# All engines' orders written out for the two MLP passes of a gated Fourier-mixing kernel

## The chip, the cores and the metric

The kernel runs on one core of one Trainium2 chip. The metric is the device time of one execution in microseconds, in fp32 throughout. The core has five engines that matter here: TensorE (PE in the profile; its weight loads are PEld), VectorE (DVE), ScalarE (ACT), GpSimd (POOL) and SyncE (SP). PE multiplies, DVE and ACT do elementwise work, SP only issues DMA transfers; POOL does here nothing but issue the transfers that add x to a tile. Each engine has its own list of instructions and waits for the others through semaphores.

## The reference, cut to what matters

```python
xn = layernorm(x)                                   # S, D = 2048, 512
a, b = xn @ dft_hid_re.T, xn @ dft_hid_im.T
s = dft_seq_re @ a - dft_seq_im @ b                 # Fourier mixing
h = relu(xn @ w1 + b1) ** 2                         # F = 1792
g = silu(h @ w2 + b2)
out = x + s * g
```

## The kernel before, in words

All matmuls work on pairs: a number is split into a high part (rounded to the matmul's fp32r type, ScalarE, line 67) and the low rest (VectorE, line 68), and each product takes the three passes high-high, high-low and low-high (PASSES). The large products are done in 2x2 blocks by a Strassen-Winograd scheme with seven products instead of eight (PRODUCTS, lines 33 to 55): sums of blocks are formed before (`sums_a`, `sums_b`), and the seven results M1 to M7 are put together after (`combine`, line 210). `combine` first copies M1 out of PSUM with ScalarE (L214) and then runs four VectorE additions (L215 to L218).

The kernel has three stages.

1. The sequence DFT (lines 300 to 613): eight chunks of 256 frequencies, ending near 419 us. Its results Y go to DRAM (`stage2`).
2. MLP pass one, `hidden`: 28 units, unit n = 7c + p for the token chunk c (4 chunks of 512 tokens) and the pair p of blocks of the hidden width (7 pairs). A unit is 42 matmuls (7 products x 2 halves x 3 passes, L474), the combine into a tile `h`, relu with b1 (L481, twice), square (L482) and a store of h to DRAM (HD, L483). Odd units use the PSUM tiles b3 and bc, even ones b2, ba and bb. In even units products 2 and 6 lie in ba, 7, 5, 3 and 4 in b2; in odd units these six lie in b3; product 1 lies in bb or bc.
3. MLP pass two, `outer`: again 28 units, 42 matmuls each (L523), which sum over p into seven PSUM tiles of chunk c (M1 in bb, M2 and M6 in b2, M7, M5 and M3 in b3, M4 in ba). Three of the tiles start from b2 (the bias): ScalarE writes it there (`bias`, L516, BIASED) ahead of the products 2, 5 and 4. After p = 6 the chunk is combined into `e` (called z in the profile), and in the next chunk's first units `finish` runs on the four parts k of z: silu (L548), times Y (L549), a transfer of GpSimd that adds x from DRAM into the tile (L552), and its store (L553). The last chunk's end is written out apart (lines 718 to 752): its last three units run product by product, and the end (`finishing`) adds x with VectorE and stores with SP.

Beside these matmuls run helpers, written as generators whose steps are placed by name with `go`: `x2` to `x7` (`xt_half`: load a raw token tile, L284; subtract the mean and multiply by the inverse deviation, L290; form sums; split), `m1` to `m3` (load the rows of means and deviations, L277), `w0`, `w4` to `w6` (`late_w2`: load a raw w2 tile, L432; form sums; split; store to DRAM, L448), `l1` to `l6` (load a finished w2 tile from DRAM, L427), and `h0` to `h27` (`operand`: load h from HD, L494; form sums; split). `beside` holds for each unit of pass one the steps ahead of it and behind it; in pass two each unit n does a step of h(n+3), h(n+2) and h(n+6).

`tc.manual_schedule` at line 618 makes VectorE and SP issue in the order in which the program is written. PE, ACT and POOL get their order from the compiler's scheduler, except in the last three units, where PE's is written too. Buffers have few homes: e (one), t (two), r (three), g1a, g1b, xc0 to xc7, wd0, wd1 and pq00 to pq11 are used by several of these steps in turn, so a load also waits until its home's former reader is done. The home of z is e: the next z can only be written when all four stores of the former z are done.

Of the kernel before, what the change touches and what calls it, by code (L numbers as in the profile page):

```python
# [9 lines left out]
AF = mybir.ActivationFunctionType  # L10
# [8 lines left out]
TC = 512  # L19
# [41 lines left out]
def fnet_gated_kernel(ctx, tc, x, xt, ct, wd, w1, w2, b1, b2, out):  # L61
# [145 lines left out]
        m26, m753, m4, m1 = ms  # L207
        return {1: m1, 4: m4, 2: m26[:, 0], 6: m26[:, 1], 7: m753[:, 0], 5: m753[:, 1], 3: m753[:, 2]}[n]

    def combine(e, ms):  # L210

        m26, m753, m4, m1 = ms
        pair = [P, 2, m1.shape[-1]]
        nc.scalar.activation(e[:, 0], m1, AF.Copy)  # L214
        nc.vector.tensor_tensor(e[:, 1:3], m26, e[:, 0:1].to_broadcast(pair), op=ALU.add)  # L215
        nc.vector.tensor_tensor(e[:, 0:4:3], m753[:, 0:2], e[:, 2:3].to_broadcast(pair), op=ALU.subtract)
        nc.vector.tensor_tensor(e[:, 2:4], m753[:, 1:3], e[:, 0:4:3], op=ALU.add)  # L217
        nc.vector.tensor_tensor(e[:, 0], m4, e[:, 0], op=ALU.subtract)  # L218
# [236 lines left out]
    def hidden(n, c, p):  # L455

        if n % 2:
            t, o = bank("b3", f"hps{n}_3"), bank("bc", f"hps{n}_1")
            t = t.rearrange("p a (b n) -> p (a b) n", n=256)
            ms = t[:, 0:2], t[:, 2:5], t[:, 5], o[:, 0, 0:256]  # L460
            order = ORDER
        else:
            t, u, o = (bank(tag, f"hps{n}_{tag}") for tag in ("b2", "ba", "bb"))
            t, u = (v.rearrange("p a (b n) -> p (a b) n", n=256) for v in (t, u))
            ms = u, t[:, 0:3], t[:, 3], o[:, 0, 0:256]
            order = ORDER if n else (1, 7, 5, 3, 4, 2, 6)
        first = set()
        for k in order:
            a, b = W1_SLOT[PRODUCTS[k][0]], B_SLOT[PRODUCTS[k][1]]

            share = next((pair for pair in ((2, 6), (7, 5), (3, 4)) if k in pair), k)
            for q in range(2):
                for a_, b_ in PASSES:
                    nc.tensor.matmul(product(ms, k), W1[p][a][:, a_, q * P:(q + 1) * P], xT[c, q][:, b_, b],  # L474
                                     start=share not in first, stop=q == 1 and (a_, b_) == (LO, HI),
                                     skip_group_check=True)
                    first.add(share)
        x_ = room(n, f"h{c}_{p}")
        combine(x_, ms)
        for f, s in ((2 * p, slice(C11, 4, 2)), (2 * p + 1, slice(C21, 4, 2))):  # L480
            nc.scalar.activation(x_[:, s], x_[:, s], AF.Relu, bias=b1s[:, f:f + 1])  # L481
        nc.scalar.activation(x_, x_, AF.Square)  # L482
        nc.scalar.dma_start(HD[c, p], x_)  # L483

    def operand(n, c, p):

# [43 lines left out]
    def at(src, k):  # L530

        h, b = WHERE[k]
        return src.rearrange("(h k p) (b e) -> h b p k e", h=2, k=2, b=2)[h, b]
# [11 lines left out]
    def finish(c, e, k):  # L545

        z = e[:, k]
        nc.scalar.activation(z, z, AF.Silu)  # L548
        nc.vector.tensor_tensor(z, z, fin[c][k // 2][:, k % 2], op=ALU.mult)  # L549
        z = z.rearrange("p (k e) -> p k e", e=256)  # L550
        tokens = slice(c * TC, (c + 1) * TC)
        nc.gpsimd.dma_start(z, at(x[tokens], k), accum_op=ALU.add)  # L552
        nc.gpsimd.dma_start(at(out[tokens], k), z)  # L553

    def finishing(c, e, k, cols=slice(0, 2)):

# [58 lines left out]
    units = [(c, p) for c in range(NTC) for p in range(NP)]  # L615
    ready, making = {}, {}

    ordered = tc.manual_schedule(engines={mybir.EngineType.DVE, mybir.EngineType.SP})

    def tokens(c, q):  # L620

# [2 lines left out]
    def go(*names):  # L624


        for v in names:
            k, n = v[0], int(v[1:])
            if k == "m":
                load_rows(n, buf("pq00", [P, 4, 256], f"rows{n}"))  # L630
            elif k == "l":
                load_w2(n)
            elif k != "h" or n < len(units):
                if v not in making:
                    making[v] = {"h": lambda: operand(n, *units[n]), "x": lambda: tokens(n // 2, n % 2),
                                 "w": lambda: late_w2(n)}[k]()
                next(making[v])
# [4 lines left out]
    def plan(c, p, ahead=(), behind=()):  # L642
        for n, names in enumerate((ahead, behind)):
            beside.setdefault((c, p), ([], []))[n].extend(names)

    for c in range(NTC - 1):
        q0, q1, w = f"x{2 * c + 2}", f"x{2 * c + 3}", f"w{NP - 3 + c}"
        late = (c == 0) * 1
        plan(*((c - 1, 4) if c else (0, 1)), [f"m{c + 1}", q0])
        plan(c, late, [q1])  # L650
        for k, p in enumerate((late, late + 1, 2)):
            plan(c, p, [], [q0])
        for p in (3, 4, 5):
            plan(c, p, [], [q1])
        plan(c, 5, [w])
        plan(c, 6, [], [w])
        plan(c + 1, 0, [], [w])
        plan(c + 1, 1, [w])
    c = NTC - 1
    plan(c, 0, ["l1", "h0"])  # L660
    plan(c, 1, ["w0"], ["h0"])
    plan(c, 2, ["h1"], ["h0", "w0"])
    plan(c, 3, [], ["w0"])
    plan(c, 4, ["l2", "h2"], ["h1"])
    plan(c, 5, [], ["h1"])
    plan(c, 6, ["h3", "l3", "h4"], ["h2"])

    with ordered:
        for n, (c, p) in enumerate(units):
            ahead, behind = beside.get((c, p), ((), ()))  # L670
            go(*ahead)
            hidden(n, c, p)
            go(*behind)
            if n == 0:
                stage2(NC - 1, 0)
                stage2(NC - 1, 1, "ba")
            if c == 0 and p + 4 < NP:
                load_w1(p + 4)

        go("h5")  # L680
        for n, (c, p) in enumerate(units):
            last = c == NTC - 1
            if p == 0:
                ms = banks(f"o{c}")
                if last:

                    m4 = bank("bc", "m_last")[:, 0], ms[2]
                for k in BIASED:
                    if last and k == 4:
                        for i in range(2):  # L690
                            bias(m4[i], k, slice(i, i + 1))
                    else:
                        bias(product(ms, k), k)
            if p == 4:
                load_fin(c)

            def add(k, p):
                if last and k == 4:
                    for i in range(2):
                        outer(m4[i], k, ready[c, p], p, (i,))  # L700
                else:
                    outer(product(ms, k), k, ready[c, p], p)

            if not last or p < REST:
                for k in NEXT if p == 0 else ORDER:
                    add(k, p)
            go(*{1: ("l4",), 3: ("l5",), 4: ("l6",)}.get(n, ()))
            go(f"h{n + 3}", f"h{n + 2}", f"h{n + 6}")
            if p == NP - 1 and not last:
                e = buf("e", [P, 4, 512], f"z{c}")  # L710
                combine(e, ms)
                done = c, e
            elif c:
                for k in ((0, 1), (2,), (3,))[p] if p < 3 else ():
                    finish(*done, k)


        e = buf("e", [P, 4, 512], f"z{c}")
        m26, m753, _, m1 = ms
        tail = NP - 1  # L720
        with tc.manual_schedule(engines={mybir.EngineType.PE}):
            for ks, ps in (((1, 2, 6), range(REST, tail)), ((1, 2, 6), (tail,)), ((7, 5, 3), range(REST, NP))):
                for k in ks:
                    for f in ps:
                        add(k, f)
            for i in range(2):
                for f in range(REST, NP):
                    outer(m4[i], 4, ready[c, f], f, (i,))
        both = slice(0, 512)

        def step(to, a, b, op, w=both):
            nc.vector.tensor_tensor(e[:, to, w], a[:, w], e[:, b, w], op=op)

        nc.scalar.activation(e[:, C21], m1, AF.Copy)
        step(C11, m26[:, 0], C21, ALU.add)
        step(C22, m26[:, 1], C21, ALU.add)
        list(finishing(c, e, C11))
        step(C21, m753[:, 0], C22, ALU.subtract)
        step(C12, m753[:, 1], C22, ALU.subtract)
        step(C22, m753[:, 1], C21, ALU.add)  # L740
        f22 = finishing(c, e, C22)
        next(f22)
        step(C12, m753[:, 2], C12, ALU.add)
        next(f22)
        f12 = finishing(c, e, C12)
        w = [slice(i * 256, (i + 1) * 256) for i in range(2)]
        step(C21, m4[0], C21, ALU.subtract, w[0])
        next(f12)
        step(C21, m4[1], C21, ALU.subtract, w[1])
        next(f12)  # L750
        for i in range(2):
            list(finishing(c, e, C21, slice(i, i + 1)))
# [43 lines left out]
```

## Time and profile before

| | us |
|---|---|
| median of 3 runs | 759.09 |
| the runs | 759.09, 759.59, 755.56 |
| the profiled execution | 755.76 |
| its span (first to last instruction) | 754.0 |
| PE busy | 712.6 (95%) |
| DVE busy | 576.9 (77%) |
| ACT busy | 347.5 (46%) |
| POOL busy | 24.3 (3%) |

A busy time is the union of an engine's instructions. PE's share is high all through, so the questions are in which stretches it is not busy, at which granted clock it runs (1.00 is full speed), and for whom it waits. In a row of the timeline stand the start in us, the length, the engine, the line, the operation, output <- input with shapes, the count, and in brackets the idle time before it with what ended it. "SPq" is SP's queue of transfers.

### The profile page before, as it was taken

The numbers are of one execution on the slowest core, as the hardware profiler recorded it, in microseconds if no ns is written. First come the engines' busy times: TensorE is split into PE (matmuls) and PEld (weight loads), VectorE is DVE, ScalarE is ACT, GpSimd is POOL, SyncE is SP. The second block draws the span as 40 slices with busy tenths as digits, with TensorE's granted clock in tenths as the row PEclk, the third lists the DMA queues.
The fourth block names the chain that finished last, engine by engine and source line by source line (L and its number), as shares of the span: only waits on it lengthen the run. The fifth ranks groups of instructions, "written<-read, shape, count | busy, mean of one in ns | idle before, by whom it ended". The sixth has DMA issues, their size and how long they took to land.

```text
span 754.0 us, 12719 instructions
## 1 busy us (share of the span) xinstructions
PE 712.6 (95%) x5149; PEld 672.1 (89%) x5149; DVE 576.9 (77%) x882; ACT 347.5 (46%) x478; POOL 24.3 (3%) x28
## 2 busy tenths in 40 slices
PE   6999999999999999999999998899999979989991
PEld 4788889999999999999999988899999979979991
DVE  7999635797796895977959529698989778768845
ACT  4437423543443544444434326575767535343511
POOL 0000000000000000000000000000000001212130
PEclk9999999999999999999999999999999999989996
DMA  8522521653835635538346677556488994828462
GB/s 308 208 93 103 196 84 51 246 180 127 294 119 195 229 129 208 188 122 279 126 148 237 232 256 256 212 187 266 177 298 307 387 366 121 248 62 245 146 159 79
DMA packets 54634, 148.43 MB, mean 197 GB/s; under 512 B 5168, under 2 KB 18992, under 8 KB 53040
## 3 DMA queue, kind: packets, MB, share of 16 engines
q1 hardware_dynamic: 46320, 126.66, 48.1%
q10 hardware_dynamic: 4032, 14.68, 4.9%
q0 software_dynamic: 4224, 6.29, 3.8%
q8 instruction: 40, 0.66, 0.3%
q14 instruction: 18, 0.15, 0.1%
HBM read 100.67 MB, written 46.94 MB: 196 GB/s over the span
## 4 chain that ended last, share of the span: by engine, by line
PE 68%; DVE 13%; DMA 11%; issue 4%; ACT 1%; SPq 1%; POOL 1%; DVEq 0%; ACTq 0%; POOLq 0%
PE m_b L265 23%; PE yps L251 12%; PE pq_b L359 7%; PE hps L474 6%; PE m_bb L265 5%; PE m_ba L265 5%; DMA z<-in_x 3%; PE hps_b L474 3%; DVE g L68 3%; PE m_b_o L523 2%; DMA xr<-in_xt 2%; DMA hr<-hd 2%; PE pq_ba L359 1%; DMA out<-z 1%; PE hps_ba L474 1%
## 5 line engine op out<-in xcount | busy, mean ns | idle before, releaser
L265 PE MATMUL m_b<-g,xc 128*128 128x256 f32 x1440 | 181.7, 281 | 0.0
L265 PEld LDWEIGHTS m_b<-g,xc 128*128 128x128 f32 x1440 | 175.7, 189 | 0.5
L523 PE MATMUL m_b_o<-w,g 128*128 128x256 f32 x840 | 108.0, 286 | 0.0
L523 PEld LDWEIGHTS m_b_o<-w,g 128*128 128x128 f32 x840 | 105.2, 195 | 0.0
L67 ACT ACTIVATE g<-r 128x768 fp32r<-128x768 f32 (+2 forms) x65 | 57.7, 889 | 97.1 <-issue 48.0
L68 DVE TENSOR_TENSOR g<-r,g 128x768 fp32r<-128x768 f32 (+2 forms) x65 | 65.4, 1007 | 43.5 <-ACT g L67 43.3
L251 PE MATMUL yps<-wd,pq 128*128 128x512 f32 x384 | 94.5, 394 | 0.0
L251 PEld LDWEIGHTS yps<-wd,pq 128*128 128x128 f32 x384 | 70.1, 188 | 14.7
L359 PE MATMUL pq_b<-g,xc 128*128 128x512 f32 x240 | 66.6, 397 | 5.0 <-ACT xc L67 4.3
L474 PE MATMUL hps<-xT,w 128*128 128x256 f32 x504 | 65.7, 286 | 4.7 <-ACT h L214 3.4
L68 DVE TENSOR_TENSOR g<-t,g 128x1024 fp32r<-128x1024 f32 x48 | 58.6, 1221 | 13.3 <-ACT g L67 13.3
L474 PEld LDWEIGHTS hps<-xT,w 128*128 128x128 f32 x504 | 63.4, 194 | 5.3 <-ACT h L214 3.6
L359 PEld LDWEIGHTS pq_b<-g,xc 128*128 128x128 f32 x240 | 44.6, 187 | 17.7 <-ACT xc L67 5.6
L67 ACT ACTIVATE g<-t 128x1024 fp32r<-128x1024 f32 x48 | 50.3, 1047 | 17.6 <-PE m_ba L265 6.9
L67 ACT ACTIVATE g<-hr 128x768 fp32r<-128x768 f32 (+1 forms) x28 | 35.4, 1266 | 37.0 <-PE m_ba_o L523 21.5
L481 ACT ACTIVATE h<-h,b1s 128x512 f32<-128x512 f32 x56 | 37.7, 715 | 28.9 <-DVE h L217 28.4
L68 DVE TENSOR_TENSOR g<-hr,g 128x768 fp32r<-128x768 f32 (+1 forms) x28 | 41.6, 1486 | 8.6 <-ACT g L67 8.6
L265 PE MATMUL m_bb<-g,xc 128*128 128x256 f32 x288 | 43.2, 282 | 0.0
L265 PE MATMUL m_ba<-g,xc 128*128 128x256 f32 x288 | 43.0, 281 | 0.0
L265 PEld LDWEIGHTS m_bb<-g,xc 128*128 128x128 f32 x288 | 39.2, 189 | 1.7
L265 PEld LDWEIGHTS m_ba<-g,xc 128*128 128x128 f32 x288 | 38.1, 189 | 0.1
L474 PE MATMUL hps_b<-xT,w 128*128 128x256 f32 x288 | 36.9, 285 | 0.0
(155 smaller groups left out, 980.7 us busy)
## 6 DMA issues: line engine op xcount, KB each, us to landing
r<-in_ct SPq DMA_DIRECT2D x63, 512.0 KB, 3.6
hd<-h ACTq DMA_DIRECT2D x28, 512.0 KB, 4.6
hr<-hd SPq DMA_DIRECT2D x28, 512.0 KB, 5.1
w1d<-w0g SPq DMA_DIRECT2D x21, 512.0 KB, 3.3
w<-w1d SPq DMA_DIRECT2D x6, 1792.0 KB, 9.0
w<-w2d SPq DMA_DIRECT2D x6, 1792.0 KB, 9.0
w2d<-w1g SPq DMA_DIRECT2D x9, 512.0 KB, 4.4
y<-ysb SPq DMA_DIRECT2D x16, 256.0 KB, 3.0
```

Source lines behind the costliest of these rows:

```text
L67: nc.scalar.activation(hi, src, AF.Copy)
L68: return nc.vector.tensor_tensor(lo, src, hi.bitcast(F32), op=ALU.subtract)
L251: nc.tensor.matmul(ps, PQ[c, m, k // 2][:, a_, w:w + P], WD[m, k][:, b_, :], start=n == 0, stop=n == 2 * ND * 3 - 1)
L265: nc.tensor.matmul(ps[:, d * CW:(d + 1) * CW], w[:, a_, d * P:(d + 1) * P], mv(b_), start=first and d == 0 and (a_, b_) == (HI, HI), stop= ...
L359: nc.tensor.matmul(accs[k], w, g[:, b_, 2 * h:2 * h + 2], start=j == 0 and h == 0 and (a_, b_) == (HI, HI), stop=j == NJ - 1 and h == 1 an ...
L474: nc.tensor.matmul(product(ms, k), W1[p][a][:, a_, q * P:(q + 1) * P], xT[c, q][:, b_, b], start=share not in first, stop=q == 1 and (a_, ...
L481: nc.scalar.activation(x_[:, s], x_[:, s], AF.Relu, bias=b1s[:, f:f + 1])
L523: nc.tensor.matmul(m[:, k * 256:(k + 1) * 256], g[:, a_, a, k * P:(k + 1) * P], W2[p][:, b_, b], start=p == 0 and k == 0 and (a_, b_) == ( ...
```

## The change

In the reduced diff below, `ordered` now covers every engine (`engines=None`), so the order of PE, ACT, DVE, POOL and SP in both passes is the order of the program text. With that the text is arranged anew:

- `hidden` yields three times. Unit n's matmuls and its copy of M1 come first, then relu, square and store of unit n-1, then the four additions of unit n, then the helpers' steps behind it.
- `finish` no longer stores. `put` does that, from SP, in the units p = 3 and p = 4 of the next chunk; all four parts of z get their silu, product and addition of x in p = 0 and p = 1 instead of p = 0, 1 and 2.
- The bias is written directly ahead of its product instead of ahead of all products of a chunk.
- In pass one, the rows and both token tiles of chunk 1 are loaded behind unit 0 (before: ahead of unit 1), a raw w2 is loaded ahead of p = 2 (before p = 5), and l3, h4, h2, h5 one unit earlier or in another order. In pass two l4, l5, l6 stand at the head of units 0, 1, 2 (before: behind the products of units 1, 3, 4), the steps of h stand between the fifth and the sixth product, and Y's loads behind p = 5 (before: ahead of p = 4).

```diff
-    def combine(e, ms):
+    def combine(e, ms, copied=False):
...
-        nc.scalar.activation(e[:, 0], m1, AF.Copy)
+        if not copied:
+            nc.scalar.activation(e[:, 0], m1, AF.Copy)
...
         x_ = room(n, f"h{c}_{p}")
-        combine(x_, ms)
+        nc.scalar.activation(x_[:, 0], ms[3], AF.Copy)
+
+        yield
+        combine(x_, ms, copied=True)
+        yield
         for f, s in ((2 * p, slice(C11, 4, 2)), (2 * p + 1, slice(C21, 4, 2))):
             nc.scalar.activation(x_[:, s], x_[:, s], AF.Relu, bias=b1s[:, f:f + 1])
         nc.scalar.activation(x_, x_, AF.Square)
         nc.scalar.dma_start(HD[c, p], x_)
+        yield
...
         nc.gpsimd.dma_start(z, at(x[tokens], k), accum_op=ALU.add)
-        nc.gpsimd.dma_start(at(out[tokens], k), z)
+
+    def put(c, e, k):
+        nc.sync.dma_start(at(out[c * TC:(c + 1) * TC], k), e[:, k].rearrange("p (k e) -> p k e", e=256))
...
-    ordered = tc.manual_schedule(engines={mybir.EngineType.DVE, mybir.EngineType.SP})
+    ordered = tc.manual_schedule(engines=None)
...
-        plan(*((c - 1, 4) if c else (0, 1)), [f"m{c + 1}", q0])
-        plan(c, late, [q1])
+        if c:
+            plan(c - 1, 4, [f"m{c + 1}", q0])
+            plan(c, 0, [q1])
+        else:
+            plan(c, 0, [], [f"m{c + 1}", q0, q1])
...
-        plan(c, 5, [w])
+        plan(c, 2, [w])
...
-    plan(c, 2, ["h1"], ["h0", "w0"])
-    plan(c, 3, [], ["w0"])
-    plan(c, 4, ["l2", "h2"], ["h1"])
-    plan(c, 5, [], ["h1"])
-    plan(c, 6, ["h3", "l3", "h4"], ["h2"])
+    plan(c, 2, ["h1"], ["h0"])
+    plan(c, 3, [], ["w0", "h1"])
+    plan(c, 4, ["l2"], ["w0"])
+    plan(c, 5, ["l3", "h4", "h2"], ["h1"])
+    plan(c, 6, ["h3", "h5"], ["h2"])
 
     with ordered:
+        before = None
         for n, (c, p) in enumerate(units):
             ahead, behind = beside.get((c, p), ((), ()))
             go(*ahead)
-            hidden(n, c, p)
+            unit = hidden(n, c, p)
+            next(unit)
+            if before:
+                next(before)
+            next(unit)
             go(*behind)
+            before = unit
...
-        go("h5")
+        next(before)
+
...
-                for k in BIASED:
+
+            def add(k, p):
+                if p == 0 and k in BIASED:
                     if last and k == 4:
                         for i in range(2):
                             bias(m4[i], k, slice(i, i + 1))
                     else:
                         bias(product(ms, k), k)
-            if p == 4:
-                load_fin(c)
-
-            def add(k, p):
                 if last and k == 4:
...
-            if not last or p < REST:
-                for k in NEXT if p == 0 else ORDER:
-                    add(k, p)
-            go(*{1: ("l4",), 3: ("l5",), 4: ("l6",)}.get(n, ()))
+            go(*{0: ("l4",), 1: ("l5",), 2: ("l6",)}.get(n, ()))
+            order = () if last and p >= REST else NEXT if p == 0 else ORDER
+            for k in order[:5]:
+                add(k, p)
             go(f"h{n + 3}", f"h{n + 2}", f"h{n + 6}")
+            for k in order[5:]:
+                add(k, p)
+            if p == NP - 2:
+                load_fin(c)
             if p == NP - 1 and not last:
                 e = buf("e", [P, 4, 512], f"z{c}")
                 combine(e, ms)
                 done = c, e
             elif c:
-                for k in ((0, 1), (2,), (3,))[p] if p < 3 else ():
+                for k in ((0, 1), (2, 3))[p] if p < 2 else ():
                     finish(*done, k)
+                for k in ((0, 1), (2, 3))[p - 3] if 3 <= p < 5 else ():
+                    put(*done, k)
```

## The prediction

> **What bounds the kernel now.** I read the page first, then the table of stretches, TensorE's waits, and last the timeline around each wait. The sum is made against the profiled execution, 755.76 us: its span and 1.76 us around it.
>
> ```profile
> span 754.0 us, 12719 instructions
> ```
>
> The MLP passes begin near 419 us. In the table of stretches a row gives length, then busy time of PE, PEld, DVE, ACT and POOL, the granted clock, DMA share and GB/s:
>
> ```profile
> 441.00:500.00 59.00, 50.83 (x401) 50.25 (x400) 42.83 (x63) 31.62 (x45) 0.00 (x0) 0.94 0.68 250
> 500.00:584.00 84.00, 82.43 (x695) 82.22 (x694) 74.70 (x111) 57.67 (x81) 0.00 (x0) 1.00 0.69 251
> 584.00:620.00 36.00, 31.27 (x245) 30.74 (x245) 27.25 (x39) 16.73 (x18) 0.00 (x0) 0.95 1.01 382
> 620.00:700.00 80.00, 76.26 (x617) 76.06 (x618) 62.72 (x80) 34.25 (x37) 16.12 (x16) 0.96 0.62 174
> ```
>
> TensorE bounds both passes, and what can be won is its idle time and lost clock. Pass one (to 584): idle 8.17 + 1.57 us, lost clock 0.06 x 50.83 = 3.05 us, together 12.8. Pass two: 584 to 620 idle 4.73 and clock 0.05 x 31.27 = 1.56, so 6.3; 620 to 700 idle 3.74 and clock 0.04 x 76.26 = 3.05, so 6.8. TensorE's own waits (total, times, longest) say who is late:
>
> ```profile
> PE m_bb_o L523 <- DMA w<-w2d: 4.7, 3, 2.6
> PE pq_b L359 <- ACT xc L67: 4.3, 3, 2.2
> PE m_bb_o L523 <- ACT z L214: 4.3, 2, 3.7
> PE hps_ba L474 <- DVE h L215: 3.5, 1, 3.5
> PE hps L474 <- ACT h L214: 3.4, 1, 3.4
> PE hps_bb L474 <- ACT h L214: 1.6, 1, 1.6
> PE hps L474 <- DVE h L218: 1.3, 1, 1.3
> ```
>
> In pass one the hps waits are for the VectorE combine (L215, L218) or for ScalarE's copy of M1 (L214), each queued behind work that waits for a load: a token tile (the DVE row below) or a raw w2. In pass two the 584-620 idle time is w2 tiles that land late; the wait on L214 (3.7, and 0.6 in a second place) is z's copy, held by the stores of the z before.
>
> ```profile
> 450.96 2.48 DVE L290 TENSOR_TENSOR xr<-xr,rows 128x1024 f32<-128x1024 f32 x2 [8.44 <-DMA xr<-in_xt]
> ```
>
> ```profile
> 606.69 2.94 SPq L542 DMA_DIRECT2D fin<-y  x4
> 609.73 0.53 SPq L427 DMA_DIRECT2D w<-w2d  x1
> ```
>
> The second fence is the last w2 load: SP issues it behind loads of Y, in the stretch whose DMA share is 1.01.
>
> **Pass one.** The token loads are issued behind unit 0, the first subtraction one unit later and raw w2 four units ahead of its splits, so the 8.44 us wait has no place; M1's copy stands ahead of the former unit's relu and square, so a late load or combine no longer holds TensorE. The cover is the second set of PSUM tiles, one unit of 42 matmuls. Matmuls follow each other in 0.12 us (the 24 from 436.77 to 439.65 below), so a unit is 5.04 us. Without that cover each late combine shows as a wait like the 3.5 above. What is late next is w1's last tile, behind the token loads on SP: 0 up to the 2.6 that a late weight cost above; I take 1.0. Net -11.8 (bounds -12.8 to -9).
>
> **The step from pass one to pass two.** With every order written out, ScalarE writes b2 into product 2's tile (L516) only after the last unit's relu and square. Today the scheduler may put it elsewhere, and no wait shows there. The chain, taken from an earlier unit:
>
> ```profile
> 436.77 3.04 PE L474 MATMUL hps<-xT,w 128*128 128x256 f32 x24
> 439.65 0.88 PE L474 MATMUL hps_bb<-xT,w 128*128 128x256 f32 x6
> ```
>
> ```profile
> 439.92 0.69 DVE L215 TENSOR_TENSOR h<-hps,h 128x512 f32<-128x512 f32 x1 [10.68 <-PE hps L474]
> 440.65 0.69 DVE L216 TENSOR_TENSOR h<-hps,h 128x512 f32<-128x512 f32 x1
> 441.37 0.69 DVE L217 TENSOR_TENSOR h<-hps,h 128x512 f32<-128x512 f32 x1
> ```
>
> ```profile
> 442.10 1.34 ACT L481 ACTIVATE h<-h,b1s 128x512 f32<-128x512 f32 x2 [1.14 <-DVE h L217]
> 443.46 1.06 ACT L482 ACTIVATE h<-h 128x1024 f32<-128x1024 f32 x1
> ```
>
> ```profile
> L516 ACT ACTIVATE m_b_o<-b2s 128x512 f32<-128x512 f32 x8 | 4.7, 591 | 4.6 <-DVE z L215 3.4 <-DVE z L217 1.2
> ```
>
> The 24 matmuls are products 7, 5, 3 and 4 of an odd unit and end at 439.81; L215 needs only 2 and 6, done before, and yet starts after the 24th: a reader waits for the whole PSUM tile. Unit 27 is odd too. So: 439.81 to 444.52 (square's end) 4.71, bias 0.59, hand-over 0.05: 5.35 us after the last hidden matmul. TensorE has only product 1 in hand, six matmuls of 0.12: a wait of 4.6. The two long waits (3.5, 3.4) made the 3.05 us of lost clock in 441-500, and one (with a 0.6) that of 620-700: 1.5 to 3.05 each; I take 2.2. The Trainium skill, "TensorE: Matmul & The Clock Gate", Part 1, says that the clock falls to half after an idle window of about 3.4 us and returns after as long a stretch of work. By that page the wait costs an estimated 1.7, and the sum would be 0.5 less. The trace differs: 584-620 loses clock (0.95) on waits of at most 2.6, so the rows are used.
>
> Bias 5 also goes into a tile behind product 3, whose reader rule it shares: 0.59, the matmuls' end (0.88 - 6 x 0.12 = 0.16) and two hand-overs of 0.05 make 0.85. Together +7.6 (4.6 to 8.5; no gain, since nothing waits here today).
>
> **Pass two.** l4, l5 and l6 (w2) go to the head of units 0, 1 and 2, l3 one hidden unit earlier, ahead of Y's loads: the 6.3 goes. The bytes stay the same and the DMA share was full, so up to 2 may remain; I take 0.5. At the three later chunk starts bias 5 costs 0.85, and bias 2 and product 7, behind z's combine, 0.4: 3 x 1.25 = +3.75. z's copy: POOL's rows show why it waits.
>
> ```profile
> 644.55 1.30 POOL L552 DMA_DIRECT2D z<-in_x  x1
> 652.65 1.22 POOL L552 DMA_DIRECT2D z<-in_x  x1 [6.80 <-issue]
> ...
> 672.97 1.23 POOL L552 DMA_DIRECT2D z<-in_x  x1 [14.68 <-DVE z L549]
> 677.56 1.23 POOL L552 DMA_DIRECT2D z<-in_x  x1 [3.36 <-issue]
> ```
>
> ```profile
> 701.59 0.60 ACT L214 ACTIVATE z<-m_bb_o 128x512 f32<-128x512 f32 x1 [3.02 <-DMA out<-z]
> ...
> 711.36 1.21 POOL L552 DMA_DIRECT2D z<-in_x  x1 [11.62 <-DVE z L549]
> ...
> 736.36 1.23 PE L523 MATMUL m_ba_o<-w,g 128*128 128x256 f32 x9
> 737.08 0.74 POOL L553 DMA_DIRECT2D out<-z  x1 [3.61 <-DMA z<-in_x]
> 739.66 0.60 ACT L734 ACTIVATE z<-m_bb_o 128x512 f32<-128x512 f32 x1 [15.13 <-DMA out<-z]
> ```
>
> An adding transfer behind another starts 4.59 us (8.10 while Y loads) after it, although it waits for nothing shown: one at a time. The stores between them add waits of their own on POOL. With the stores on SP I take a cycle of 5.0, near 4.59, because Y's loads move to unit 5. Four cycles and a store (2.1 below, with issue 2.5) free z 22.5 us after the first addition; now it is 739.66 - 711.36 = 28.3. It is needed 7 x 5.04 - (711.36 - 701.59) = 25.5 after it, so the 6.8, and 0.5 of the small wait at 701.59, go. SP blocks on each of these stores, with h's loads behind it; they are issued six units early and used three later, so this is hidden. Sum of pass two: -6.3 + 0.5 + 3.75 - 7.3 = -9.35.
>
> **The tail.** From the last matmul group's end, 737.59, to 754.0 is 16.4 us, because the last combine's copy (739.66) waits for the same stores. It comes 5.8 earlier. But the final loads of Y and x now stand behind the stores on SP:
>
> ```profile
> fin<-y SPq DMA_DIRECT2D x4, 256.0 KB, 3.8
> out<-z POOLq DMA_DIRECT2D x4, 256.0 KB, 3.8
> fin<-in_x SPq DMA_DIRECT2D x4, 256.0 KB, 6.6
> out<-z SPq DMA_DIRECT2D x3, 256.0 KB, 2.1
> ```
>
> The first x piece used is the sixth of eight, issued 0.5 us apart: 20 + 0.4 + 5 x 0.5 = 22.9, landed at 26.7 (3.8) or 29.5 (6.6). The add is ready 22.5 + 0.6 + 3 x 0.7 = 25.2 after the first addition: 1.5 to 4.3 late; I take 2.0, near the row of the less crowded loads. Net -3.8 (-7 to 0).
>
> **Sum.** -11.8 + 7.6 - 9.35 - 3.8 = -17.35: 755.76 becomes 738.4. The three runs of before give 755.56, 759.09 and 759.59, so the profiled one lies 3.3 below their median; half of that added, I say 740.0.
>
> **Rivals.** (a) The moved stores bring nothing. The Trainium skill's opening page, "Trainium Kernel Development and Optimization", Key Constraints, says that transfers issued from SP, ACT and POOL share the same 16 DMA engines and that a second issuer saves only issue time. As a mechanism here: z stays late by as much as now, 7.3 + 3.8 back, 751.1. For it: the same bytes; against it: POOL's idle 6.80 and 3.36 us lie in its own queue. 0.08. (b) w2 isn't really earlier, because SP, in order, still waits for h's buffers ahead of l4: 6.3 back, 746.3. 0.07. (c) VectorE becomes pass one's bound. It was busy 42.83 + 74.70 = 117.5 of the 143 us from 441 to 584; with 12.8 us gone that is 117.5 of 130.2. If its idle share stays as it is, since splits wait for ScalarE, 11.8 comes back: 751.8. For it: 89% in the stretch 500-584, which has one wait of 1.6. 0.15. (d) Slower: additions cycle at 8.10 everywhere. z is then free 34.9 after the first, 5 later than the 25.5 plus the one unit that TensorE still has; with clock about 7.5 at two chunk ends, 15, and 4 x 3.1 = 12.4 at the end: 767. This decides from a cycle of about 7.5 up. Against it: that row ran beside Y's loads. 0.10.
>
> **How the numbers follow.** Forecast 0.60. A measurement here can tell about 0.5%, 3.8 us, from no change. Faster by more (below 755.3): the forecast, (a), (b), and half of (c), whose bounds reach 756: 0.82. Same: the other half of (c), and a little of (d) where the cycle is near 7.5: 0.10; slower 0.08. The forecast's bounds are -10 (clock, tail, pass one at their best) and +10; with (a), (b) and most of (c) inside, the range is 730 to 755.
>
> **What would show it.** Right: no hps wait over 1 us before the last unit; one wait of 4 to 5 us on ACT L516 at the pass change, and a dip in PEclk after it; no m_bb_o wait on w2d or on z; four additions at about 5 us; L734 before the last matmul ends and a tail near 12 us. Wrong: hps waits on L215 or L218 in mid-pass (c), additions over 7 us apart (d), m_bb_o waiting for w2d (b).

## The result, and the profile after

| | before | after |
|---|---|---|
| median, us (4 runs each) | 759.34 | 735.36 |
| the runs, us | 755.56 to 766.58 | 734.07 to 737.00 |
| profiled execution, its span | 755.76, 754.0 | 734.07, 732.3 |
| last matmul group's end in the span | 737.59 | 722.5 |
| from there to the span's end | 16.4 | 9.8 |
| DVE busy | 576.9 | 576.9 |
| POOL busy | 24.3 | 14.9 |

The ratio is 0.9674 (95% interval 0.9599 to 0.9749): faster, by 24.0 us of the medians and 21.7 us of the spans. Line numbers of the changed kernel: M1's copy L480, `combine` L216 to L219, relu L486, square L487, the store of h L488, bias L522, outer matmul L529, Y's product L555, the addition of x L558, `put` L561, the last z's copy L755.

TensorE's waits after the change (total, times, longest), all of those in the MLP passes:

```profile
PE m_b_o L529 <- ACT m_b_o L522: 7.9, 5, 5.2
...
PE m_b_o L529 <- DVE z L218: 0.3, 1, 0.3
```

The hps rows, the w2d row and the row of z's copy are gone. What is left is the bias, and one wait of 0.3 us for z's combine. The table of stretches (length, then busy PE, PEld, DVE, ACT, POOL, granted clock, DMA share, GB/s):

```profile
441.00:500.00 59.00, 59.00 (x500) 59.00 (x499) 55.07 (x81) 41.02 (x57) 0.00 (x0) 1.00 0.80 291
500.00:584.00 84.00, 78.16 (x637) 77.75 (x636) 71.47 (x107) 57.05 (x77) 0.00 (x0) 0.96 0.78 298
584.00:620.00 36.00, 35.27 (x294) 34.89 (x293) 27.34 (x33) 15.42 (x18) 0.00 (x0) 1.00 0.56 203
620.00:700.00 80.00, 78.21 (x647) 77.26 (x647) 69.26 (x92) 38.21 (x44) 12.32 (x10) 1.00 0.71 185
```

The first row has no idle time and the full clock. All that the second one loses, 5.84 us idle and 0.04 x 78.16 = 3.1 us of clock, lies at the change of passes. The timeline there:

```profile
569.26 0.87 PE L529 MATMUL m_bb_o<-w,g 128*128 128x256 f32 x6
...
570.97 0.69 DVE L218 TENSOR_TENSOR h<-hps,h 128x512 f32<-128x512 f32 x1
...
571.69 1.33 ACT L486 ACTIVATE h<-h,b1s 128x512 f32<-128x512 f32 x2 [2.57 <-DVE h L218]
...
573.06 1.06 ACT L487 ACTIVATE h<-h 128x1024 f32<-128x1024 f32 x1
...
574.26 0.33 ACTq L488 DMA_DIRECT2D hd<-h  x1
574.63 0.60 ACT L522 ACTIVATE m_b_o<-b2s 128x512 f32<-128x512 f32 x1 [0.51 <-DMA hr<-hd]
...
575.28 5.30 PE L529 MATMUL m_b_o<-w,g 128*128 128x256 f32 x24 [5.15 <-ACT m_b_o L522]
...
581.28 0.98 PE L529 MATMUL m_b_o<-w,g 128*128 128x256 f32 x6 [0.69 <-ACT m_b_o L522]
```

TensorE waits 5.15 us for a bias that stands behind combine, relu, square and the store's issue; the 24 matmuls behind it take 5.30 us instead of the 3.04 quoted above, so 2.26 are lost clock (from 575.2 to 580.6 us the granted clock was 0.53); with the 0.69 us for bias 5 that is 8.1. GpSimd's additions of the last chunk, and the tail:

```profile
693.58 1.21 POOL L558 DMA_DIRECT2D z<-in_x  x1 [18.00 <-DVE z L555]
698.56 1.22 POOL L558 DMA_DIRECT2D z<-in_x  x1 [3.77 <-DVE z L555]
703.09 1.21 POOL L558 DMA_DIRECT2D z<-in_x  x1 [3.31 <-DVE hs L184]
707.75 1.22 POOL L558 DMA_DIRECT2D z<-in_x  x1 [3.45 <-issue]
```

```profile
714.93 0.60 ACT L755 ACTIVATE z<-m_bb_o 128x512 f32<-128x512 f32 x1 [5.50 <-DMA out<-z]
...
720.96 0.69 DVE L571 TENSOR_TENSOR z<-z,fin 128x512 f32<-128x512 f32 x1 [3.22 <-DMA fin<-in_x]
721.27 1.23 PE L529 MATMUL m_ba_o<-w,g 128*128 128x256 f32 x9
```

The additions go 4.5 to 5.0 us apart, z is copied 21.35 us after the first one and 7.6 us ahead of TensorE's end (before: 2.1 behind it), and x's first piece comes 3.22 us late.

### The profile page after: what moved, and what is told of

Its sections match the earlier page's. It is cut to its first block, busy times and chain, and to the rows that moved or that the text cites. A ratio compares the mean times of both kernels' runs of the same rounds, so it can differ in the third digit from the quotient of the medians.

```text
span 732.3 us, 12730 instructions
## 1 busy us (share of the span) xinstructions
PE 709.3 (97%) x5149; PEld 668.2 (91%) x5149; DVE 576.9 (79%) x882; ACT 349.8 (48%) x478; POOL 14.9 (2%) x16
## 4 chain that ended last, share of the span: by engine, by line
PE 83%; DVE 9%; DMA 3%; issue 2%; ACT 1%; SPq 1%; POOL 0%; DVEq 0%; ACTq 0%; POOLq 0%
PE m_b L266 23%; PE yps L252 12%; PE hps L475 8%; PE m_b_o L529 8%; PE pq_b L360 7%; PE m_bb L266 5%; PE hps_b L475 5%; PE m_ba L266 5%; PE hps_ba L475 2%; DVE g L68 2%; PE m_ba_o L529 2%; PE pq_ba L360 2%; PE m_bb_o L529 1%; DMA hr<-hd 1%; PE hps_bb L475 1%
## 5 line engine op out<-in xcount | busy, mean ns | idle before, releaser
L529 PE MATMUL m_b_o<-w,g 128*128 128x256 f32 x840 | 108.7, 287 | 8.4 <-ACT m_b_o L522 7.9
L529 PEld LDWEIGHTS m_b_o<-w,g 128*128 128x128 f32 x840 | 104.7, 194 | 10.1 <-ACT m_b_o L522 9.1
L252 PEld LDWEIGHTS yps<-wd,pq 128*128 128x128 f32 x384 | 70.2, 188 | 14.9
L475 PE MATMUL hps<-xT,w 128*128 128x256 f32 x504 | 61.9, 281 | 0.0
L475 PEld LDWEIGHTS hps<-xT,w 128*128 128x128 f32 x504 | 60.9, 190 | 0.1
L68 DVE TENSOR_TENSOR g<-hr,g 128x768 fp32r<-128x768 f32 (+1 forms) x28 | 41.6, 1487 | 11.1 <-ACT g L67 11.1
L486 ACT ACTIVATE h<-h,b1s 128x512 f32<-128x512 f32 x56 | 37.4, 716 | 21.0 <-DVE h L218 21.0
```

What stands on the lines that cost most here:

```text
L68: return nc.vector.tensor_tensor(lo, src, hi.bitcast(F32), op=ALU.subtract)
L252: nc.tensor.matmul(ps, PQ[c, m, k // 2][:, a_, w:w + P], WD[m, k][:, b_, :], start=n == 0, stop=n == 2 * ND * 3 - 1)
L529: nc.tensor.matmul(m[:, k * 256:(k + 1) * 256], g[:, a_, a, k * P:(k + 1) * P], W2[p][:, b_, b], start=p == 0 and k == 0 and (a_, b_) == ( ...
```

## The experiments

**Theory**: the gain is four waits taken away (late loads in pass one, w2 behind Y's loads, the stores between GpSimd's additions, the tail behind the same stores), and ScalarE's written order gives 8 us back at the change of passes. **Rivals**: the written order itself brings the gain; or the moved transfers bring nothing, since the bytes stay the same. Twelve kernels were run. The kernels in the first group were timed beside a before of 762.27 us (17 runs), the second 762.29 (13), the third 761.48 (11). Before's own runs spread from 755.6 to 767.5, the changed kernel's over 3 us, so I compare medians with the changed kernel's 735.36, give the ratio to before, and settle what is under 3 us by parts of the spans. The changed kernel itself was timed only beside the 759.34 above.

### w2 alone, in the kernel before

```diff
-    plan(c, 5, [], ["h1"])
-    plan(c, 6, ["h3", "l3", "h4"], ["h2"])
+    plan(c, 5, ["l3"], ["h1"])
+    plan(c, 6, ["h3", "h4"], ["h2"])
...
+            go(*{0: ("l4",), 1: ("l5",), 2: ("l6",)}.get(n, ()))
             if not last or p < REST:
                 for k in NEXT if p == 0 else ORDER:
                     add(k, p)
-            go(*{1: ("l4",), 3: ("l5",), 4: ("l6",)}.get(n, ()))
```

> The kernel before with one part of the change alone: l4, l5, l6 at the head of units 0, 1, 2 of pass two and l3 one hidden unit earlier. My theory (w2 was late because it stood behind Y's loads on SP): no wait of TensorE on w2d in 584-620 us, -5.8 us, so about 753.5 beside 759.3 for before. Rival b (the bytes land no earlier, since SP waits for h's buffers ahead of l4, or since the stretch is full): the waits on w2d stay at 3 us or more, and the time is within 1 us of before.

758.23 us, ratio 0.9959 (0.9937 to 0.9981): about 4 us instead of 5.8. TensorE's waits:

```profile
PE m_bb_o L523 <- ACT z L214: 11.2, 2, 5.8
PE hps_ba L474 <- DVE h L215: 4.1, 1, 4.1
```

No wait on w2d is left, so rival b is out: the loads are really earlier. But the wait for z's copy, 4.3 us in the quoted profile of before, is now 11.2. The matmuls of a chunk that starts earlier reach its end earlier, and the stores that hold z there don't move with them (GpSimd's last stores of the first two chunks are issued at 658.06 and 698.79 us, before at 657.53 and 698.99): part of the gain is given back at the next bound. How large a part the two profiles can't say, since before's is among its quickest and this one is 3.0 us longer than it. The term is worth its size only together with the stores.

### Stores alone, in the kernel before

```diff
-        nc.gpsimd.dma_start(at(out[tokens], k), z)
+
+    def put(c, e, k):
+        nc.sync.dma_start(at(out[c * TC:(c + 1) * TC], k), e[:, k].rearrange("p (k e) -> p k e", e=256))
...
-            if p == 4:
-                load_fin(c)
...
+            if p == NP - 2:
+                load_fin(c)
...
-                for k in ((0, 1), (2,), (3,))[p] if p < 3 else ():
+                for k in ((0, 1), (2, 3))[p] if p < 2 else ():
                     finish(*done, k)
+                for k in ((0, 1), (2, 3))[p - 3] if 3 <= p < 5 else ():
+                    put(*done, k)
```

> The kernel before with the stores alone moved: all four parts of z finished in p = 0 and 1, stored from SP in p = 3 and 4, Y loaded behind p = 5. My theory (GpSimd issues one thing at a time, so stores between the additions hold the next addition): additions 4.5 to 6 us apart, the waits on z's copy (4.3 us) and their lost clock (3) gone and the tail 4 to 6.6 us shorter, -11 to -14, so 745 to 748 beside 759.3. Rival a (the same bytes through the same engines): within 1 us of before. Rival d (additions 8 us apart): the same or slower.

743.27 us, ratio 0.9769 (0.9739 to 0.9799): 19 us of the medians, 10.6 of the spans (743.4 against 754.0; that profile of before is among its quickest runs). TensorE's waits:

```profile
PE m_bb_o L523 <- DMA w<-w2d: 2.8, 2, 2.7
...
PE m_bb_o L523 <- ACT z L214: 0.3, 1, 0.3
```

z's wait falls from 4.3 to 0.3 and the tail to 743.4 - 731.5 = 11.9. Rival a is out, and this part alone brings far more than w2 alone; by the medians it is also more than the 11 to 14 us that I expected. It isn't the stores by themselves, though: the edit moves Y's loads as well, and with chunk 0's Y now behind the last w2 load the wait on w2d falls from 4.7 to 2.8.

### The changed kernel with its stores back on GpSimd

```diff
         nc.gpsimd.dma_start(z, at(x[tokens], k), accum_op=ALU.add)
+        nc.gpsimd.dma_start(at(out[tokens], k), z)
...
-                for k in ((0, 1), (2, 3))[p - 3] if 3 <= p < 5 else ():
-                    put(*done, k)
```

> The changed kernel with the stores put back on GpSimd, each behind its addition, and none on SP. My theory: the cycle of an addition and a store is 5.5 to 6.5 us instead of 4.5 to 5.3, so z comes free 3 to 5 us later, which costs 0 to 2 us at the two chunk ends (they have some us to spare) and 2 to 4 us in the tail, less the 3.2 us for which the tail waits for x today, since SP is then free for the last loads: +0 to +6 against the changed kernel's 735.4. Rival a (the place of the stores is worth nothing): within 1 us of 735.4. If the forecast's whole 11.1 us hang on the queue, as the prediction had it: 746.

748.59 us, ratio 0.9830 (0.9805 to 0.9855): 13.2 us slower than the changed kernel. My expectation here was too low. GpSimd in the last chunk:

```profile
703.62 1.21 POOL L558 DMA_DIRECT2D z<-in_x  x1 [14.64 <-DVE z L555]
710.91 0.75 POOL L559 DMA_DIRECT2D out<-z  x1 [6.09 <-DMA z<-in_x]
711.66 1.25 POOL L558 DMA_DIRECT2D z<-in_x  x1
719.47 0.75 POOL L559 DMA_DIRECT2D out<-z  x1 [6.57 <-DMA z<-in_x]
```

```profile
731.30 1.23 PE L529 MATMUL m_ba_o<-w,g 128*128 128x256 f32 x9
732.98 0.60 ACT L754 ACTIVATE z<-m_bb_o 128x512 f32<-128x512 f32 x1 [13.51 <-DMA out<-z]
```

```profile
PE m_bb_o L529 <- ACT z L215: 4.0, 2, 3.5
```

Each store waits on GpSimd for its addition to land, with the next addition queued behind it: 8.0 us for the first pair. The last z's copy comes 29.4 us after the first addition and behind TensorE's end (732.53), and the tail is 747.3 - 732.53 = 14.8 (+5.0). In mid-pass TensorE waits 4.0 us for z's copy again (the third fence), and loses 2.8 us of clock after the longer of these waits. Neither chunk end had the slack that I counted on. Of the 15.0 us between the spans, 1.8 lie at the change of passes (a wait of 6.71 instead of 5.15 and a little more clock), where nothing was edited; without them the queue cost some 13 by the spans, beside the prediction's 11.1.

### TensorE, ScalarE and GpSimd ordered by the scheduler

```diff
-    ordered = tc.manual_schedule(engines=None)
+    ordered = tc.manual_schedule(engines={mybir.EngineType.DVE, mybir.EngineType.SP})
```

> The changed kernel's text with only VectorE's and SP's order taken from it; TensorE's, ScalarE's and GpSimd's are the scheduler's, as before. Theory 1 (the gain comes from loads and stores put elsewhere, and the written order itself costs the 8 us at the change of passes): 726 to 730, no wait on the bias, no hps waits over 1 us. Theory 2 (the written order of ScalarE brings pass one's gain): hps waits on M1's copy return with 4 us or more, the wait on the bias goes, 732 to 740.

728.29 us, ratio 0.9570 (0.9542 to 0.9599): 7.1 us quicker than the changed kernel. All of TensorE's waits in the passes:

```profile
PE m_bb_o L529 <- ACT g L67: 0.9, 2, 0.5
PE m_b_o L529 <- ACT m_b_o L522: 0.7, 1, 0.7
```

So the rival that the written order brings the gain is out. The loads and stores bring it, as VectorE and SP issue them in the new text; the order written out for TensorE, ScalarE and GpSimd costs about what the change of passes costs. No hps wait is left here either, although the scheduler sets ScalarE's order: with the early loads, pass one doesn't need M1's copy to be written ahead of relu and square. (The text still has it first; whether that guides the scheduler was not tried.)

### Chunk 0's biases ahead of the last unit's relu

```diff
+        ms = banks("o0")
+        for k in BIASED:
+            bias(product(ms, k), k)
         next(before)
```

> The changed kernel with chunk 0's three biases written by ScalarE ahead of the last hidden unit's relu instead of behind its square and store. My theory (the wait at the change of passes is ScalarE's order alone, 5.15 + 0.69 us, and the 2.26 us of lost clock are its consequence): the wait on the bias at the change shrinks to 1 us or less, the 24 matmuls behind it take 3 to 3.5 us, -5.5 to -8: 727.5 to 730. Rival (TensorE isn't fed there anyway: operands of h or w2 come next): -2 or less, 733.5 or more, with a new wait in its place.

728.90 us, ratio 0.9573 (0.9542 to 0.9605): -6.5 as expected; by the spans -5.0 (732.3 to 727.3). The longest wait on L522 is 1.0 us, and the granted clock behind it is 1.00. With the scheduler's kernel, this shows the pass change by removal.

### The last chunk's x early

```diff
             if p == NP - 2:
                 load_fin(c)
+                if c == NTC - 2:
+                    load_fin(NTC - 1, (1,))
```

`load_fin` is given which of Y and x to load; the line added loads x alone.

> The changed kernel with the last chunk's four loads of x issued behind Y's loads of the chunk before, so that they don't stand behind the stores. My theory (the tail waits 3.2 us for x, which stands behind the stores on SP): no wait of VectorE on x in the tail, -2 to -3.5, 732 to 733.4. Rival (the tail is bound by the chain behind the last matmul, and x is covered): within 0.7 us of 735.4.

733.31 us, ratio 0.9635 (0.9605 to 0.9665): -2.1. In the span only the tail can tell: 731.8 - 723.14 = 8.7 instead of 9.8, so 1.1 of the 3.2 us. VectorE no longer waits for x, but now for TensorE:

```profile
713.03 7.98 PE L529 MATMUL m_b_o<-w,g 128*128 128x256 f32 x66
...
720.84 1.23 PE L529 MATMUL m_last<-w,g 128*128 128x256 f32 x9
721.04 2.02 DVE L757 TENSOR_TENSOR z<-m_b_o,z 128x512 f32<-128x512 f32 x3 [0.57 <-PE m_b_o L529]
```

The tile of products 7, 5 and 3 ends at 721.01 (the first row), and VectorE's chain behind it sets the tail: both answers were partly right.

### Pass one's loads back

```diff
-        if c:
-            plan(c - 1, 4, [f"m{c + 1}", q0])
-            plan(c, 0, [q1])
-        else:
-            plan(c, 0, [], [f"m{c + 1}", q0, q1])
+        plan(*((c - 1, 4) if c else (0, 1)), [f"m{c + 1}", q0])
+        plan(c, late, [q1])
...
-        plan(c, 2, [w])
+        plan(c, 5, [w])
```

> The changed kernel with pass one's loads put back: the rows and token tiles of chunk 1 ahead of unit 1, a raw w2 ahead of p = 5. M1's copy stays ahead of relu and square. My theory as the prediction had it (an early load and an early copy each remove a part: the load the waits on VectorE's combine, 3.5 + 1.3 us, the copy those on M1, 5.0): hps waits on the combine return with 3 to 6 us and 1 to 3 us of clock, 739 to 744. Rival 1 (the copy alone does it): within 1 us of 735.4. Rival 2 (the loads alone do it): 745 or more.

742.46 us, ratio 0.9748 (0.9713 to 0.9783): +7.1, within my theory's band. TensorE in pass one:

```profile
453.35 2.04 PE L475 MATMUL hps_ba<-xT,w 128*128 128x256 f32 x12 [2.68 <-DVE h L216]
455.42 4.22 PE L475 MATMUL hps_b<-xT,w 128*128 128x256 f32 x24
...
461.81 4.55 PE L475 MATMUL hps<-xT,w 128*128 128x256 f32 x36 [1.45 <-DVE h L219]
```

The two waits on the combine come back, those on M1's copy (3.4 and 1.6 before) don't. That shows the first half of the prediction's pass one, the loads. The second half, the copy, is the next kernel.

### M1's copy behind relu and square

```diff
-        nc.scalar.activation(x_[:, 0], ms[3], AF.Copy)
-
         yield
-        combine(x_, ms, copied=True)
+        combine(x_, ms)
```

The copy is then made by `combine`, behind the former unit's square.

> The changed kernel with M1's copy of unit n behind relu and square of unit n-1 again, the loads early as in the change. My theory (relu and square hold ScalarE for 2.4 us and the second set of tiles covers 5): mid-pass no wait, and at the change of passes nothing moves: within 1 us of 735.4. Rival (the copy's place carries pass one's gain): hps waits on M1's copy or the combine behind it, +3 to +8, 738 to 743.

755.67 us, ratio 0.9920 (0.9894 to 0.9946): +20.3, far beyond what any theory said. ScalarE's timeline:

```profile
527.44 0.38 ACT L215 ACTIVATE h<-hps_bb 128x256 f32<-128x256 f32 x1 [0.46 <-ACT h L486]
...
530.11 1.34 ACT L485 ACTIVATE h<-h,b1s 128x512 f32<-128x512 f32 x2 [0.60 <-DVE h L218]
531.48 1.06 ACT L486 ACTIVATE h<-h 128x1024 f32<-128x1024 f32 x1
...
533.00 0.38 ACT L215 ACTIVATE h<-hps 128x256 f32<-128x256 f32 x1 [0.46 <-ACT h L486]
...
538.48 0.38 ACT L215 ACTIVATE h<-hps_bb 128x256 f32<-128x256 f32 x1 [0.46 <-ACT h L486]
```

The copies come 5.5 us apart. Copy n starts VectorE's combine n; relu n waits for that combine; copy n+1 waits behind relu and square n. The two engines now work in turn, and a round of 5.5 us is longer than a unit of 5.04. My "2.4 us against a cover of 5" counted one engine's work and not the loop through two. In pass one TensorE waits for the combine (L219, 6.6 us in all) and for token splits that come late on VectorE (4.9). Its first outer matmul starts at 584.68 instead of 569.26, 15.4 us later, and the wait behind it is 8.65 us instead of 5.15:

```profile
594.20 5.49 PE L528 MATMUL m_b_o<-w,g 128*128 128x256 f32 x24 [8.65 <-DVE hs L185]
```

The row names VectorE's hs, which ended 0.04 us after the bias (594.18 and 594.14). Together that is 18.9 of the span's 20.4.

### Y's loads beside the additions

```diff
-            if p == NP - 2:
+            if p == (2 if c else NP - 2):
                 load_fin(c)
```

> The changed kernel with Y's loads behind unit p = 2 of chunks 1 to 3 instead of p = 5, so that they run beside the four additions. Rival d of the prediction (the cycle beside Y's loads is 8.1 us, that is what made before's additions slow): second and third cycle 7 us or more, z free 27 us or more after the first addition, waits of TensorE on z's copy and a longer tail, +5 to +15. My reading of the changed kernel's trace (its cycles of 7.4 to 7.8 us ran without Y's loads, beside stores and h's loads, so Y is not the cause by itself): the first three cycles stay under 6 us and the time within 3 us of 735.4, or below it, as Y and x no longer stand behind the stores.

739.50 us, ratio 0.9722 (0.9667 to 0.9777): +4.1, between the two. In the last chunk:

```profile
697.04 1.21 POOL L558 DMA_DIRECT2D z<-in_x  x1 [16.90 <-DVE z L555]
704.39 1.22 POOL L558 DMA_DIRECT2D z<-in_x  x1 [6.13 <-DVE hr L185]
712.54 1.21 POOL L558 DMA_DIRECT2D z<-in_x  x1 [6.92 <-issue]
717.14 1.22 POOL L558 DMA_DIRECT2D z<-in_x  x1 [3.39 <-issue]
```

Beside loads of Y and x the cycle is 7.35 and 8.15, so that row of before was read rightly; z's copy still costs TensorE no wait, and the tail is 737.7 - 725.97 = 11.7 (+1.9). Of the rest of the span's +5.4, 1.1 lie at the change of passes, whose wait is 6.49 in this profile with 0.2 less clock lost behind it, and 1.7 in longer waits at the last two chunk starts. But the changed kernel has cycles of 7.37 and 7.84 too, in chunks 1 and 2, beside its stores and no load of Y. So Y isn't the only traffic beside which a cycle is long; which traffic counts was not taken apart.

### All biases at the chunk's head, and x early

```diff
             if p == 0 and c:
                 ms = banks(f"o{c}")
...
+                for k in BIASED:
+                    if last and k == 4:
+                        for i in range(2):
+                            bias(m4[i], k, slice(i, i + 1))
+                    else:
+                        bias(product(ms, k), k)
...
-                if p == 0 and k in BIASED:
...
```

The lines for chunk 0's biases and for x are those shown above.

> The changed kernel with all biases written at the head of their chunk, chunk 0's ahead of the last hidden unit's relu, and the last chunk's x loaded behind the Y of the chunk before. If the terms add (7.5 for the change of passes, 3 for x, 1 to 2.5 for the biases of the three later chunks): ratio to before 0.950 to 0.955, 722 to 725. If ScalarE's three biases in a row only move the wait to the products behind them: 726 to 728.

726.89 us, ratio 0.9547 (0.9514 to 0.9580): the ratio lies at the upper end of the first case's, the time in the second's band, and the cause is the second's. TensorE's waits at the four chunk starts are 1.00, 0.65, 0.95 and 0.96; at the later three the changed kernel has 0.69, 0.69 and 1.04 (0.35 + 0.69). Product 7 now waits for bias 5, and the three later chunks win nothing.

### The scheduler's order, and x early

```diff
-    ordered = tc.manual_schedule(engines=None)
+    ordered = tc.manual_schedule(engines={mybir.EngineType.DVE, mybir.EngineType.SP})
...
                 load_fin(c)
+                if c == NTC - 2:
+                    load_fin(NTC - 1, (1,))
```

> The changed kernel's text with TensorE's, ScalarE's and GpSimd's order left to the scheduler, and the last chunk's x loaded behind the Y of the chunk before. If the tail's wait for x is separate from the order of the passes: 3 us less than the same kernel without the early x (ratio to before 0.957), so 0.953, with no wait on x in the tail. If the scheduler fills that time otherwise: 0.957.

724.60 us, ratio 0.9518 (0.9486 to 0.9550): the quickest of all, 10.8 us under the changed kernel. Against the same kernel without early x it is -3.7 in medians and -1.9 in spans; the tail is 722.8 - 714.19 = 8.6.

### More space for GpSimd's descriptors

```diff
-    b2s = pool.tile([P, D], F32, name="b2s")
...
-        nc.scalar.activation(m, b2s[:, None, b:b + 256]...
+        nc.scalar.activation(m, b1s[:, None, 0:1]...
...
-    ... dynamic_dma_scratch_size=1024)
+    ... dynamic_dma_scratch_size=3072)
```

> The changed kernel with the space for the descriptors of GpSimd's transfers 3072 instead of 1024 bytes a partition; to make room b2's tile is left out and the bias is written from the first column of b1, so the output lacks b2 and the instructions stay the same. Theory (additions go one at a time because the space holds the descriptors of little more than one): additions are issued 1.2 to 3 us apart, z is free 10 to 14 us after the first, the tail is 3 to 4 us shorter, 731 to 733. Rival (one at a time for another reason, such as the shared home or the order of sums in memory): cycles of 4.5 to 7.8 us as in the changed kernel, within 1 us of 735.4.

734.28 us, ratio 0.9643 (0.9603 to 0.9683); this kernel leaves b2 out of its output. GpSimd, two additions to a row:

```profile
695.48 2.44 POOL L555 DMA_DIRECT2D z<-in_x  x2 [29.76 <-DVE z L552]
700.21 2.46 POOL L555 DMA_DIRECT2D z<-in_x  x2 [2.29 <-DVE z L552]
```

SP's stores, with the last z's copy, in this kernel, and then the stores in the changed one:

```profile
699.93 8.32 SPq L558 DMA_DIRECT2D out<-z  x4
...
714.55 0.60 ACT L752 ACTIVATE z<-m_bb_o 128x512 f32<-128x512 f32 x1 [3.15 <-PE m_bb_o L526]
```

```profile
698.30 14.17 SPq L561 DMA_DIRECT2D out<-z  x4
```

The second addition follows the first at once: that they went one at a time was the space for descriptors. SP has issued the last store 12.8 us after the first addition (708.25) instead of 18.9 (712.47), and z's copy waits for TensorE (the row of L752) and no longer for stores. The mechanism was as my theory had it, the price was not: it is worth 1.2 us of the tail (733.1 - 724.46 = 8.6), the same floor as with early x, set by VectorE's chain behind the last tiles.

## Why the prediction was right

It said 740.0, the measured median is 735.36, inside 730 to 755. The terms against what the two profiles show:

| step | forecast | measured | by |
|---|---|---|---|
| pass one | -11.8 | -12.8 | no loss is left up to the last unit |
| change of passes | +7.6 | +8.1 | 5.15 + 2.26 + 0.69 |
| pass two | -9.35 | -10.6 | 6.3 + 6.8 lost before, 0.73 + 1.79 after |
| tail | -3.8 | -6.6 | 16.4 to 9.8 |
| sum | -17.35 | -21.9 | the spans differ by 21.7 |

The gain is 4.5 us larger than forecast, 2.8 of it in the tail.

- **Pass one** held. With the loads back, which cost 7.1, the waits on the combine returned and those on M1's copy stayed away, as it said. The 1.0 for w1's last tile did not come (in the kernel with more descriptor space it did, as 0.9). Two things it had wrong or missed. It gave the copy's place a part of the gain, but in the scheduler's kernel the early loads alone leave no hps wait. And once the order is written, the copy's place carries 20 us, through a loop of ScalarE and VectorE that the prediction never counted. It was safe here because the change made both edits.
- **The change of passes** held in place, chain and size: a wait of 4.6 forecast, 5.15 measured, the difference the issue of h's store ahead of the bias; 2.2 of clock against 2.26. Removing the cause brought 6.5.
- **w2**: the 5.8 is about right in the changed kernel, where 0.73 of the 6.3 lost in 584 to 620 are left and 0.69 of that is a bias. It is wrong as a term by itself: alone it gave about 4, and z's wait grew instead. The prediction added terms that share a bound.
- **The stores**: 11.1 for the queue stands beside 13.2 by putting them back. The cycle of 5.0 held in the last chunk (4.98, 4.53 and 4.66), but not in chunks 1 and 2, where it was 6.0 and 5.9 in the mean with one addition over 7 us each, the sign that the prediction gave for rival d. In chunk 1 z came free 25.6 us after the first addition (ScalarE's copy at 646.64 waited 0.38 for the stores), not 22.5. TensorE didn't wait, because it needed that tile only at 649.17, 1.9 us after the copy's end: here the term came out with little room, and partly by luck.
- **Three chunk starts**: +3.75 forecast, 2.4 measured (0.69, 0.69, 0.35 + 0.69). The 0.4 for product 7 came once, not three times.
- **The tail** is the term most mis-sized: "z free 22.5 us after the first addition" was 21.35, and x, taken as 2.0 late, was 3.22 late; that these two nearly cancel is luck. What failed is the count from TensorE's end. The additions started 28.9 us ahead of that end (722.5 - 693.58), not 26.2 as before (737.59 - 711.36), so z's copy came 7.6 us ahead of it and left the path; the tail then met a floor of 8.6 us, which four kernels show (x early, both edits, the scheduler with x early, more descriptor space), and x's 3.2 us cost only 1.2.

Rivals (a) and (b) are shown false by the stores and by w2 alone. Rival (c), VectorE as pass one's bound, did not come: it was busy 55.07 of 59.00 us there and TensorE had no wait. That share, 93%, says that this bound is close by.

## What to carry to other kernels

Before you write out an in-order engine's order, follow each pair of engines that hand work to each other round by round: if A waits for B's work on item n before it does the step of item n+1 that B waits for, the round trip is the bound, however idle both look. Where a gain comes from loads and stores, make that edit with the scheduler's order left alone as well; here the written order cost 7 of the some 33 us that the moved transfers won (0.9570 of 759.34). A wait removed upstream is worth its size only if the next bound moves too, so try the terms alone and together.

## What the runs showed of the hardware that was not expected

- **An addition in flight fills GpSimd's space for descriptors.** With 1024 bytes a partition the additions are issued 4.5 us apart at best, even where the profile shows no releaser but "issue" or an unrelated row; with 3072 two are issued within 2.44. The Trainium skill, "DMA: Bandwidth & Descriptors", section on SWDGE, HWDGE and iDMA, says that GpSimd writes the descriptors into rings in a part of SBUF set aside; "SBUF — State Buffer", section on its size, gives 16 KiB a partition for it. This kernel had cut it to 1 KiB. With 3 KiB the tail is 1.2 us shorter.
- **The clock drops after waits of 1.8 to 8.7 us, and the loss doesn't follow their length.** After 2.68 us (the row of loads back, above) 12 and 24 matmuls took 2.04 and 4.22 us instead of some 1.6 and 3.04, so about 1.6 are lost; after 3.45 (stores back on GpSimd) 6 and 24 took 1.65 and 5.09 instead of 0.88 and 3.04, so 2.8; after 5.15, 2.26; after 8.65 24 took 5.49, so 2.45. Behind waits of 0.69 and 0.98 us the granted clock stayed at 1.00. The kernel with M1's copy behind has two waits of nearly one length, with 38 matmuls behind each:

```profile
468.05 4.74 PE L475 MATMUL hps<-xT,w 128*128 128x256 f32 x38 [1.75 <-DVE xT L68]
...
547.97 6.27 PE L475 MATMUL hps<-xT,w 128*128 128x256 f32 x38 [1.81 <-DVE xT L68]
```

  Behind the first the granted clock was 1.00, behind the second 0.73, and 1.5 us were lost. The Trainium skill's "TensorE: Matmul & The Clock Gate", Part 1, has an idle window of about 3.4 us; by these runs 1.8 is enough at times.
- **The wait at the change of passes isn't fixed.** It was 5.15 in the changed kernel, 6.71 with the stores back on GpSimd, 6.49 with Y beside the additions, though nothing before it was edited. The profile names a load of h as what ScalarE waits for there (0.51 us in the row of L522 above, 2.07 in the second kernel). Why a bias or the store ahead of it should wait for that load was not tried and stays open.
